# Attention with routed clusters, then a Fourier gate: the first head pair set ahead of the Fourier tables

## The chip, the cores and the metric

The kernel runs on one core of one Trainium2 chip. A core has five engines that work side by side: TensorE (PE) multiplies matrices and loads its weights beside that (PEld), VectorE (DVE) and ScalarE (ACT) work on elements and empty the accumulation banks, GpSimd (POOL) does small things in on-chip memory, and SyncE (SP) issues transfers. ACT and POOL can issue transfers too. The metric is the device time of one launch in microseconds (us), the median of several runs; lower is better. Profile times count from the first instruction of one profiled execution.

## The reference

There are 4 batches of 8 heads, 768 positions of 64 numbers. Each position of q and of k is assigned to one of 16 centroids of its head, by the largest cosine. Attention is allowed only between positions of the same centroid. The result, 768 x 512 per batch, goes through a projection to three parts, a circular convolution of the second with a filter (by Fourier transform), a product with the other two parts and an output projection.

```python
mask = q_assign[:, :, :, None] == k_assign[:, :, None, :]
scores = np.where(mask, scale * np.matmul(q, k.transpose(0, 1, 3, 2)), -1e9)
attn = softmax(scores); x = heads_side_by_side(np.matmul(attn, v))
x1, x2, x3 = split(x @ w_proj)
x2_conv = irfft(rfft(x2) * rfft(filter_fft))
out = (x1 * x2_conv * x3) @ w_out
```

## The kernel before, in words

**Attention.** Heads come in groups n of four (two groups to a batch), each in two pairs pr = 0, 1. A pair takes six steps sk, one for each 128 keys. A step has three score products of 512 columns (L660, issued by `product` as one matmul of 128 weight columns, L72, or two of 64, L74), three exponentials on ACT into one of five p buffers (L669, L672), eight matmuls of P.V into a bank pair (L683), and an addition of p on DVE for the row sums (L697). The mask rides inside the score product: 16 rows below q and k hold the centroid as a one-hot row, times a large number for q, so that unequal centroids give a hugely negative score. These rows are the tiles `augm`; the 64 rows of data are `aug`, cast to bf16.

**Routing.** For each group the q and k tiles are loaded (L295), transposed by PE (L556, or L566 for groups 0 and 1), copied out, multiplied with normalised centroids (`sim`), transposed back, and turned into one-hot rows by five DVE operations. For group 0 this is `first_masks` (L467): once per pair, the keys (j = 1) and queries (j = 0) of both heads together. Pair 0's rows are written by PE transposes and copies (L511, L520); pair 1's go through a tile `ohT` and four transfers issued by SP (L462).

**Fourier tables.** `angles` (L337) makes 768-point angles on DVE with exact rounding, and their sines on ACT into `fw`. `tables` (L375) transposes them into `inv`, loads the filter (L381), and works out the filter's spectrum (L418 to L440). Before, the sines are among the first things on ACT, and every first exponential is made to wait for the last of them by `after=sins`. The second half of the kernel, `hyena` (L785), uses `fw`, `inv` and the spectrum `hm` for each batch.

**The order.** Nothing is ordered by hand. `build` lists some 1,900 operations with the engines that may run them, an estimated duration, a due time and their data dependencies. `Plan.place` (L113) then simulates the engines: of the operations that are ready at about the earliest time, it takes on each engine the one with the smallest due time, with bonuses for staying with P.V and penalties for changing the column mode of PE. Each engine's instructions are issued in the order that comes out. Due times follow a raster: `T0` for the first step, `TAU1` per step for the first 28 and `TAU2` after. `NUDGE` adds a correction to the due time of single operations by their number in the list. A load is not issued earlier than `LEAD` ahead of its due time. Transfers of group 0's heads may go by SP or by ACT; the rest by SP, in order.

```python
o.due += NUDGE.get(o.seq, 0.0)
if o.kind == "load":
    o.ready = max(o.ready, o.due - LEAD)
T0 = 20.38450
TAU1 = 2.97769
```

Of the kernel before, what the change touches and what calls it, by code (L numbers as in the profile page):

```python
# [75 lines left out]

class Plan:

    def __init__(self):
        self.ops, self.writers, self.reads = [], {}, {}

    def op(self, eng, fn, due, r=(), w=(), alloc=None, free=(), lock=False, byts=0, after=(), kind=None, lat=0.0):
        o = Op()
        o.eng = eng if isinstance(eng, dict) else {eng[0]: eng[1]}
        o.fn, o.due, o.alloc, o.free, o.lock, o.byts, o.kind = fn, due, alloc, free, lock, byts, kind
        o.seq = len(self.ops)
        o.due += NUDGE.get(o.seq, 0.0)
        o.outs, o.end, o.start, o.on = [], None, None, None  # L90
        deps, o.soft = set(after), set(after)
        o.lat = lat
        for key in r:
            deps.update(self.writers.get(key, ()))
        for key in w:
            deps.update(self.writers.get(key, ()))
            deps.update(self.reads.get(key, ()))
        for key in r:
            self.reads.setdefault(key, []).append(o)
        for key in w:  # L100
            self.writers[key] = [o]
            self.reads[key] = []
        deps.discard(o)
        o.deps = deps
        o.left = len(deps)
        for d in deps:
            d.outs.append(o)
        for h in free:
            h.readers += 1
        self.ops.append(o)  # L110
        return o
# [107 lines left out]
def banks_for(bank, free, st, o):  # L219
# [14 lines left out]
    elif st.o == st.otiles:  # L234
        if st.tail:
            allowed += [4, 5]
        elif whole(4, 6) < 1e8:
            first += [4, 5]
    t = lambda i: whole(4, 6) if i in first else free[i]
    ids = sorted((i for i in allowed + first if free[i] < 1e8), key=lambda i: (t(i), i))[:bank.n]  # L240
    return (tuple(ids), max(map(t, ids))) if len(ids) == bank.n else None


def build(T):

    P = Plan()
    op = P.op
    T0 = 20.38450
    TAU1 = 2.97769
    TAU2 = 3.43320  # L250
    NE = 28

    def ring(n, pr):
        return (2 * n + pr) % 3

    def A(i):
        return T0 + TAU1 * min(i, NE) + TAU2 * max(i - NE, 0)

    def copy(e, out, in_):
        if e == "ACT":  # L260
# [915 lines left out]
```

## Time and profile before

| | |
|---|---|
| runs shown, median (lowest to highest) | 387.03 us (386.67 to 388.61), 3 runs |
| profiled execution: span | 385.4 us (its own device time is not listed; the median lies 1.6 us above the span) |
| PE busy | 367.3 us |
| DVE busy | 352.3 us |
| ACT busy | 273.1 us |
| POOL busy | 46.6 us |
| first matmul, first exponential, end of the last matmul | 5.11, 22.39, 381.0 us |

The page of a profile gives busy time per engine and, in its fourth part, the chain of work that ended last, followed back from the end. A view by stage gives busy time in chosen stretches. The timeline lists instructions in order of time, merged where like follows like: start, duration, engine, line, operation, output <- input, partitions x elements, count, and in brackets the idle time before and what ended it. PE counts as busy while any matmul is in flight, so a busy PE can be a slow one; the duration of equal instructions tells.

### The profile page before, as it was taken

The page shows a single profiled execution, that of the slowest core. Times are in us where ns is not written, and L with a number is a line of the kernel's source. Part 1 is how long each engine was busy: PE and PEld are TensorE (multiplying, and loading weights), DVE is VectorE, ACT ScalarE, POOL GpSimd, SP SyncE. Part 2 cuts the span into 40 slices and gives each one's busy share as a digit, 9 for nine tenths or more (in the row PEclk, how much of TensorE's full clock was granted, in tenths as well). Part 3 has the DMA queues.
Part 4 walks back from the last instruction along what each step waited for, and adds up shares of the span by engine and source line. Part 5 has one row for each costly group of instructions (what it writes and reads, how often), then busy time and mean ns, then how long its engine had stood idle before and what let it go on. Part 6 is the DMA issues. An engine that isn't in the chain of part 4 may idle for free.

```text
span 385.4 us, 8486 instructions
## 1 busy us (share of the span) xinstructions
PE 367.3 (95%) x3262; PEld 207.6 (54%) x3267; DVE 352.3 (91%) x504; ACT 273.1 (71%) x519; POOL 46.6 (12%) x92
## 2 busy tenths in 40 slices
PE   2999899999999999989999999999999999999995
PEld 1564345445655555556555555555455566555682
DVE  8898988998798999998899999999998999999883
ACT  5897987887894979577975967687867367532342
POOL 8602000000012010101010100101010100000400
PEclk9999999999999999999999999999999999999999
DMA  9819984730679669767886896645657551010214
GB/s 176 196 52 216 215 182 120 170 72 22 166 146 187 119 119 143 121 113 126 161 104 174 144 246 108 119 88 91 102 102 198 62 115 43 4 43 2 101 67 163
DMA packets 93860, 47.17 MB, mean 122 GB/s; under 512 B 82088, under 2 KB 87676, under 8 KB 93820
## 3 DMA queue, kind: packets, MB, share of 16 engines
q1 hardware_dynamic: 87836, 36.84, 42.5%
q0 software_dynamic: 2704, 8.98, 16.0%
q10 hardware_dynamic: 3280, 0.82, 1.2%
q8 instruction: 25, 0.41, 0.5%
q14 instruction: 15, 0.12, 0.1%
HBM read 31.59 MB, written 7.40 MB: 101 GB/s over the span
## 4 chain that ended last, share of the span: by engine, by line
PE 65%; DVE 19%; ACT 6%; issue 4%; DMA 3%; SPq 1%; POOL 0%; DVEq 0%; ACTq 0%; POOLq 0%
PE bank L74 24%; PE pair L683 21%; DVE acc L697 6%; PE bank L809 5%; PE bank L72 4%; PE bank L556 3%; ACT p L672 2%; PE bank L586 2%; DMA dr<-dn 2%; DMA aug<-ohT 2%; ACT aug L261 2%; DVE tm L833 2%; PE bank L599 1%; PE bank L451 1%; PE bank L566 1%
## 5 line engine op out<-in xcount | busy, mean ns | idle before, releaser
L683 PE MATMUL pair<-p,vraw 128*64 128x385 f32 x768 | 142.5, 490 | 0.2
L672 ACT ACTIVATE p<-bank 128x512 f32<-128x512 f32 x192 | 113.7, 613 | 34.1 <-PE bank L74 29.3
L697 DVE TENSOR_TENSOR acc<-p,acc 128x1536 f32<-128x1536 f32 x64 | 112.0, 1750 | 3.9 <-ACT p L672 1.5
L683 PEld LDWEIGHTS pair<-p,vraw 128*64 128x64 f32 x768 | 54.2, 136 | 47.8 <-issue 41.1
L74 PE MATMUL bank<-aug,aug 128*64 128x512 bf16 (+3 forms) x580 | 68.4, 328 | 2.1 <-ACT p L672 1.2
L669 ACT ACTIVATE p<-bank 128x512 f32<-128x512 f32 x96 | 58.6, 611 | 6.2 <-PE bank L74 5.6
L74 PEld LDWEIGHTS <-aug 128*64 128x64 bf16 (+1 forms) x580 | 34.4, 109 | 34.5 <-issue 22.4
L731 POOL DMA_DIRECT2D acc<-acc x30 | 23.6, 788 | 242.6 <-DMA acc<-acc 90.3
L74 PE MATMUL bank<-xT,wpj 128*64 128x384 bf16 x440 | 42.7, 326 | 0.0
L261 ACT COPY qkT<-bank 128x384 f32<-128x384 f32 x63 | 28.1, 497 | 10.5 <-PE bank L74 8.9
L74 PEld LDWEIGHTS <-wpj 128*64 128x64 bf16 x440 | 25.5, 109 | 15.9 <-issue 6.4
L697 DVE TENSOR_TENSOR acc<-p,p 128x1536 f32<-128x1536 f32 x16 | 28.0, 1751 | 3.3 <-ACT p L672 3.1
L74 PEld LDWEIGHTS <-y 128*64 128x64 bf16 x464 | 22.9, 110 | 12.6 <-issue 4.4
L261 ACT CAST aug<-qkT 64x768 bf16<-64x768 f32 x33 | 27.3, 829 | 2.5 <-PE bank L74 1.7
L833 DVE TENSOR_TENSOR tm<-bank,hm 128x512 f32<-128x512 f32 x44 | 27.7, 678 | 0.1
L809 PE MATMUL bank<-wpj,xT 128*64 128x512 bf16 x192 | 21.9, 379 | 0.0
L74 PE MATMUL bank<-wout,y 128*64 128x512 bf16 x176 | 21.1, 379 | 0.0
L72 PE MATMUL bank<-aug,aug 80*128 80x256 bf16 (+3 forms) x92 | 20.0, 321 | 0.2
L556 PE MATMUL bank<-ident,qkraw 128*128 128x128 f32 x144 | 19.6, 279 | 0.3 <-DVE sd L898 0.3
L556 PEld LDWEIGHTS bank<-ident,qkraw 128*128 128x128 f32 x144 | 15.6, 140 | 6.9 <-issue 4.5
L261 ACT COPY tm<-bank 128x512 f32<-128x512 f32 x13 | 7.4, 589 | 15.8 <-PE bank L809 12.0
L701 ACT COPY osb<-pair 128x770 f32<-128x770 f32 x16 | 12.9, 809 | 6.9 <-PE pair L683 6.8
(150 smaller groups left out, 433.0 us busy)
## 6 DMA issues: line engine op xcount, KB each, us to landing
vraw<-in_v_dram SPq DMA_DIRECT2D x16, 384.0 KB, 4.3
qkraw<-in_q_dram SPq DMA_DIRECT2D x30, 192.0 KB, 4.1
qkraw<-in_k_dram SPq DMA_DIRECT2D x30, 192.0 KB, 4.1
rb<-dr SPq DMA_DIRECT2D x30, 192.0 KB, 3.7
out_dram<-ob SPq DMA_DIRECT2D x11, 512.0 KB, 3.0
acc<-acc POOLq DMA_DIRECT2D x10, 384.0 KB, 6.2
acc<-acc POOLq DMA_DIRECT2D x10, 192.0 KB, 4.2
y<-in_moe_filter_fft_dram SPq DMA_DIRECT2D x4, 384.0 KB, 7.1
```

The lines of the kernel that those rows point to most:

```text
L72: return T.nc.tensor.matmul(out, lhsT, rhs, start=start, stop=stop)
L74: T.nc.tensor.matmul(out[64 * i:64 * i + 64], lhsT[:, 64 * i:64 * i + 64], rhs, start=start, stop=stop)
L261: T.nc.scalar.copy(out, in_)
L556: T.nc.tensor.transpose(bank(h.ids[i // 3])[:, ts(i % 3, 128)], raw(s, i), T.ident)
L669: T.nc.scalar.activation(o, ap(h).rearrange("p (a b) -> p a b", a=2), Act.Exp, scale=0.125)
L672: T.nc.scalar.activation(flat(s)[:, lo:lo + 512], ap(h), Act.Exp, scale=0.125)
L683: T.nc.tensor.matmul(o[64 * hp:64 * hp + 64, ch, :385], T.vraw[vs][:, hp, sk * D:(sk + 1) * D], T.p[slots[sk]][:, hp, 384 * ch:384 * ch + ...
L697: T.nc.vector.tensor_tensor(T.acc[os], P_(t[0]), P_(t[1]) if len(t) == 2 else T.acc[os], op=Alu.add)
L701: op(("ACT", .83), lambda e: T.nc.scalar.copy(T.osb[o3], two(ob)[:, :, :385]), te, r=[ob], w=[("osb", o3)], free=[ob])
L731: op(("POOL", .8), lambda e, rows=rows: T.nc.gpsimd.dma_start(flat_()[:rows], flat_()[rows:2 * rows], accum_op=Alu.add), te, r=[], w=[("ac ...
L809: T.nc.tensor.matmul(ap(h)[64 * i:64 * i + 64], T.xT[xs][:, kt, c:c + 64], T.wpj[:, kt, DM:2 * DM], start=kt == 0, stop=kt == ND - 1)
L833: op(("DVE", .68), lambda e, i=i, cs=cs, r=r, h=h: T.nc.vector.tensor_tensor(T.tm[r][:, cs], ap(h), hmrow(i, (0, 2, 2, 3)[2 * r + cs]), op ...
```

## The change

Six things change.

1. *Loads.* The four head loads of pair 0 come first, two on SP and two on ACT; pair 1's four go to SP, with later due times. The loads of the following groups and of the filter no longer wait for the first masks.
2. *Centroids.* A dummy square root and, after the real one, a dummy exponential are put on ACT, so that their function tables are loaded there. The first exponential depends on the latter instead of on the sines.
3. *First masks.* `first_masks(pr, js)` works for pair 0 once for the keys and once for the queries, each with both halves of the positions in one bank, and for pair 1 once for both. The factor of the query rows moves into the constant that marks ties, so that the rows come out by one subtraction (queries) or comparison (keys). Pair 1's masks take eight transfers instead of four.
4. *Angles, sines, tables.* They are listed after the first pair's attention. The angles wait for the first exponential; all sines are one operation on ACT, with the table loads for sine and back to exponential, after the sixth exponential. Tables, filter loads and spectrum get due times relative to `T0`.
5. *Constants.* `T0` is 13.0. Two zero fills of pair 0's tiles go to DVE; the column constants of the old masks go.
6. *Order.* `NUDGE` has 1,911 entries (mean size 133 us) instead of 271 (mean size 2.4 us). A new table `ONLY` pins 160 operations to one engine: 98 to ACT, 51 to DVE, 11 to POOL.

```diff
-NUDGE = {6:-0.2,9:0.7,10:3.7,11:-0.3,71:-0.3, ...
+NUDGE = {0:11.4019,1:487.416,2:-43.9661,3:160.599, ...
+ONLY = {9:"POOL",10:"POOL",11:"POOL",39:"POOL",40:"POOL",50:"DVE",54:"DVE",56:"ACT", ...
...
+        if o.seq in ONLY:
+            o.eng = {ONLY[o.seq]: o.eng[ONLY[o.seq]]}
...
-    T0 = 20.38450
+    T0 = 13.0
...
+    ANG, SINES, LOADF, TAB = T0 + 6, T0 + 10, T0 + 14, T0 + 20
...
-        return [op({"SP": .8, "ACT": .8} if n == 0 else ("SP", .8), lambda e, hp=hp: dma(e)(
+        return [op(("ACT" if hp and (n, pr) == (0, 0) else "SP", .65), lambda e, hp=hp: dma(e)(
...
-        sq = op(("ACT", 1.5), lambda e: T.nc.scalar.activation(cen.s0, cen.ss, Act.Sqrt), 2.4, r=["ss"], w=["s0"])
+        op(("DVE", .1), lambda e: V().memset(T.warm, 1.0), -3, w=["warm"])
+        op(("ACT", 1.45), lambda e: T.nc.scalar.activation(T.warm, T.warm, Act.Sqrt), 1.0, w=["warm"])
+        sq = op(("ACT", .2), lambda e: T.nc.scalar.activation(cen.s0, cen.ss, Act.Sqrt), 2.4, r=["ss", "warm"], w=["s0"])
+        ex = op(("ACT", 1.45), lambda e: T.nc.scalar.activation(T.warm, T.warm, Act.Exp), 2.5, w=["warm"], after=[sq])
...
+        def sines(e):
+            A_ = T.nc.scalar.activation
+            for m, n, r in todo:
+                A_(T.fw[:, :, m, 192:], n(), Act.Sin, scale=sc)
+                A_(T.fw[:, :, m, :192], r(), Act.Sin, scale=sc, bias=T.half_pi)
+            A_(T.ph[:, 0], T.kp, Act.Sin, scale=-math.pi / S, bias=T.half_pi)
+            A_(T.ph[:, 1], T.kp, Act.Sin, scale=math.pi / S)
+            A_(T.warm, T.half_pi, Act.Exp)
+        op(("ACT", 6.5), sines, SINES, r=keys + ["kp", "half_pi"], w=[("fw", m, cs) for m in range(3) for cs in range(2)] + ["ph", "warm"],
+           after=[exps[5]])
...
-    def first_masks(pr):
+    def first_masks(pr, js):
...
+        def pick(e):
+            for z in js:
+                x = oh().rearrange("p (t j m) c -> p t j m c", j=w_, m=4)[:, :, z - js[0]]
+                y = m2().rearrange("p (t j m) -> p t j m", j=w_, m=4)[:, :, z - js[0]]
+                V().tensor_tensor(x, x, y.unsqueeze(3).to_broadcast([128, 3, 4, NC]), op=Alu.is_equal if z else Alu.subtract)
...
-                        free=[h], after=sins if first[0] is None else [first[0]], kind="exp")
+                        free=[h], after=[warm] if first[0] is None else [first[0]], kind="exp")
...
-    for z in range(4):
-        load_qk(0, z // 2, z % 2, .3 + z * .1)
-    sins = angles(sq)
-    got = routing(0)
-    load_v(0, 0, 2.0)
-    for z in range(4):
-        load_qk(1, z // 2, z % 2, 9 + z)
-    load_v(0, 1, 20)
-    tables(got)
+    for z in range(2):
+        load_qk(0, 0, z, .3 + z * .1)
+    load_v(0, 0, 8.0)
+    for z in range(2):
+        load_qk(0, 1, z, 6.5 + z * .1)
+    routing(0)
+    for z in range(4):
+        load_qk(1, z // 2, z % 2, 12 + z)
+    load_v(0, 1, 18)
     for n in range(NG):
-        attention(n, 0, sins)
+        attention(n, 0)
+        if n == 0:
+            angles()
+            tables()
```

## The prediction

> **What bounds the kernel now.** I read the first page for the busy shares, then the busy time by stage, then the timeline of the first 25 us engine by engine, and last the chain of work that ended last. From the page:
>
> ```profile
> span 385.4 us, 8486 instructions
> PE 367.3 (95%) x3262; PEld 207.6 (54%) x3267; DVE 352.3 (91%) x504; ACT 273.1 (71%) x519; POOL 46.6 (12%) x92
> PE 65%; DVE 19%; ACT 6%; issue 4%; DMA 3%; SPq 1%; POOL 0%; DVEq 0%; ACTq 0%; POOLq 0%
> ```
>
> TensorE (PE) is busy 95% of the span and carries 65% of the chain; VectorE (DVE) is close behind. A busy PE may still be a slow one, so the stages come next: start and length, then the busy time of PE, PE's weight loads, DVE, ScalarE (ACT) and GpSimd (POOL), granted clock, DMA share, GB/s.
>
> ```profile
> 0.00:5.11 5.11, 0.00 (x1) 0.03 (x1) 3.61 (x13) 0.78 (x1) 4.18 (x25) 1.00 0.60 134
> 5.11:10.21 5.10, 2.38 (x9) 1.61 (x9) 4.90 (x11) 4.55 (x9) 4.88 (x15) 1.00 1.31 233
> 10.21:22.40 12.19, 12.19 (x96) 7.54 (x97) 10.79 (x23) 10.77 (x22) 5.39 (x13) 1.00 0.74 172
> 22.40:100.00 77.60, 74.68 (x578) 38.30 (x579) 67.33 (x84) 64.73 (x126) 2.61 (x5) 1.00 0.62 134
> 100.00:350.00 250.00, 247.05 (x2190) 139.82 (x2190) 239.97 (x335) 180.36 (x342) 24.46 (x31) 1.00 0.63 118
> 350.00:385.40 35.40, 30.99 (x398) 20.32 (x394) 25.66 (x43) 11.86 (x23) 5.08 (x4) 0.98 0.23 90
> ```
>
> From 22.4 us, where the first exponential starts, to 350 us PE idles 2.92 + 2.95 us in all. So the time is PE's work plus what PE loses at the two ends. The start, as the timelines give it:
>
> ```profile
> 4.33 1.28 ACT L315 ACT_TABLE_LOAD   x1 [4.33 <-issue]
> 5.85 1.28 ACT L358 ACT_TABLE_LOAD   x1
> 15.81 1.28 ACT L372 ACT_TABLE_LOAD   x1
> 22.39 0.58 ACT L672 ACTIVATE p<-bank 128x512 f32<-128x512 f32 x1
> ...
> 5.11 1.51 PE L566 MATMUL bank<-ident,qkraw 128*128 128x128 f32 x6 [5.11 <-DMA qkraw<-in_q_dram]
> 7.61 0.87 PE L566 MATMUL bank<-ident,qkraw 128*128 128x128 f32 x3 [0.99 <-DMA qkraw<-in_k_dram]
> 10.21 0.42 PE L326 MATMUL bank<-ident,sd 128*64 128x128 f32 x1 [1.73 <-DVE sd L323]
> 12.48 2.76 PE L477 MATMUL bank<-qkT,cbd 128*32 128x384 f32 x8
> 16.67 1.48 PE L477 MATMUL bank<-qkT,cbd 128*32 128x384 f32 x8
> ```
>
> Keys land at 7.6 us; centroids are normalised only by 10.2, because DVE works on the angles in between; similarities come at 12.5; and the sine work on ACT (7.1 to 17.3) stands before the first exponential by an explicit dependency. The same eight similarities take 2.76 us, then 1.48: PE runs slowly at first, although the granted clock reads 1.00. The transposes of L566, first those of 5 to 12 us, then those of 18 to 24 us (min/median/max in ns), say the same:
>
> ```profile
> L566 PE MATMUL bank<-ident,qkraw x17: 417/421/448, 5.1 to 11.9; 128*128 128x128 f32 x17
> L566 PE MATMUL bank<-ident,qkraw x15: 272/273/328, 18.3 to 22.3; 128*128 128x128 f32 x15
> ```
>
> **The change part by part.** The start in PE's ledger first. By 22.4 us PE has done, at later rates: 39 transposes at 0.122 us (L556, 12 in 1.46 us) = 4.8; 16 similarities at 0.089 (16 of L586 in 1.43) = 1.4; the small transposes L487 (0.58 per six), L393 (0.33 per three) and L511 (24 in 0.84) = 3.3; the rest 0.6. That is 10.1 us of work, so PE is 12.3 us behind.
>
> *Loads.* Four head loads (q and k of pair 0, 192 KB each) now stand first, two on SP and two on ACT; before, eight shared the 16 DMA engines. At the 217 GB/s that the trace shows from 3 to 9 us, four take 3.6 us from about 2.5, so keys land at 6.1; the upper bound is 7.6, as now. Three issues on ACT instead of five free it at 1.16 + 0.65 + 0.67 = 2.5 instead of 4.3. SP issues the rest: the second pair's four, v, then the next heads' eight, 0.65 each, 9 us of a queue that idles from 18.0 to 25.07 now. The eight mask issues in place of four add 4 x 0.63 = 2.5 us there; what waits behind them, the filter loads and the third heads' loads, is used from 45 us on. No charge; if that cover is gone, 2.5.
>
> *Centroids.* The square root's table (1.28) loads while the centroids fly, so the root is out near 4.1 instead of 5.8. The five small DVE operations that follow (8.28 to 10.16 now) lose the angles from between them: about 1.2 us. Transpose 0.42, two copies 0.45: ready by 6.9, before the keys' transposes are copied out. Nothing is added to the chain.
>
> *First mask.* From keys at 6.1: two groups of three transposes at the slow 0.87 each, 7.9; copy 0.48, 8.4; four similarities, half of 2.76, 9.8; copy 0.47, 10.3; transposes 0.4, 10.7; five DVE operations on half as many elements, between half and all of 0.55 + 0.56 + 0.36 + 0.55 + 0.56 = 2.6, I take 1.6 for 12.3; the queries' own five stand partly in between, +0.7, 13.0; row transposes 0.3, copy 0.8, score 0.4, gaps 0.2: first exponential at 14.7, 7.7 earlier. By then PE has done 12 transposes (1.5), similarities and small transposes 2.1, the rest 0.6, and in its waits the second pair's 12 (1.5) and six of the next heads' (0.7): 6.4 us, so it is 8.3 behind. **Gain 12.3 - 8.3 = 4.0 us.** The other 3.7 us of the 7.7 are PE work that is still to be done, and PE has no idle time behind it to hide it in.
>
> *Angles and sines.* Twelve DVE operations cost 7.9 us now, 0.36 to 0.98 each, the long ones beside POOL's memsets; undisturbed 3 x (0.36 + 0.36 + 0.56 + 0.56) = 5.5. DVE idles 10.3 us from 22.4 to 100, which covers them; uncovered they cost 5.5. The sines become one block on ACT among the exponentials: 3 x 0.52 + 3 x 0.62 + 0.30 + 0.19 + two table loads 2.56 + 0.20 = 6.7 us. The bounds are 0 and 6.7. Covered are up to four filled p buffers at 1.30 us of P.V each, 5.2; I take 6.7 - 5.2 = **+1.5**. The Trainium skill ("ScalarE: Activation LUTs", What ACT_TABLE_LOAD costs) states a further 1.38 us of drain per switch of set; by that the block would last 9.4 us and the sum would be 2.7 us higher; the trace disagrees where it can be seen, the load at 5.85 starts 0.02 us after the root ends at 5.83.
>
> *Memsets and small things.* Two zero fills move from POOL (0.79) to DVE in the first 2 us, where DVE waits 1.34 us for the identity; the DVE price is not in the trace, between 0.15 and 0.56 (its shortest operation and the cast of that shape). Off the path, nothing.
>
> *The order.* The list of due-time corrections grows from 271 small entries (2.4 us in the mean) to one for nearly every operation (133 us in the mean), and 160 operations are pinned to one engine. Every choice among ready operations can differ. What can be priced is the column mode of PE: a P.V step of eight takes 1.30 us after its like and 1.45 after another mode, as the chain shows:
>
> ```profile
> 138.68 2.17 PE bank L72 x13
> 140.85 1.45 PE pair L683 x8
> 142.51 1.30 PE pair L683 x8
> ```
>
> I count 85 changes of mode between 0 and 345 us in PE's timeline, 48 of them before 130 us; after that 11 or 12 in each 70 us. The bounds: all of the early excess gone, 28 x 0.15 = -4.2; the count doubled, 85 x 0.15 = +12.8. Neither end is near to a row, but the early stretch is the one that is rebuilt, and it has the room; I take half of the lower, **-2.1**. PE's idle time of 5.9 us in the middle I leave.
>
> Sum, against the profiled execution: 385.4 - 4.0 + 1.5 - 2.1 = 380.8 of span. The profiled execution lists its span alone; the 1.6 us from there to the median of the runs (387.03) I take as what lies around the span: **382.4**.
>
> **The rivals.** (B) *The whole 7.7 us are kept.* From 36.7 to 52 us the chain runs through ACT and DVE (four aug casts of 0.83, a 1.75 accumulate, the filter's scalings), not PE; if these two set the early pace, all shifts. Against: PE idles only 2.9 us up to 100. 387.0 - 7.7 + 1.5 - 2.1 = 378.7. (C) *The sine block is uncovered:* scores stop, P.V has nothing in stock; all 6.7 are paid: 387.6. For: ACT is busy 64.7 of 77.6 us there. (E) *PE stays slow.* It works in short pieces up to 14.7 us, so the slow pace (421 against 273 ns) may last into the first scores; it lasted some 7 us from PE's first matmul before, and if 5 us of them fall behind the first score at half rate, that is +2.5: 384.9. The Trainium skill ("TensorE: Matmul & The Clock Gate", Part 1) gives such a rule: half clock until a window of about 3.4 us has been busy. The trace agrees, as PE turns fast between 12 and 15 us only. (D) *Slower than before: the new order changes column mode more often*, all along the span. Without the -2.1 the sum is 384.5; it passes 389.0 with (389.0 - 384.5) / 0.15 = 30 more changes; with 50 it gives 392.0, doubled 397.3. For it speaks that 250 us of the span are at 99% PE, where a rearrangement can hardly win; against, that the modes' price is among what the planner weighs.
>
> **How the numbers follow.** Likeliest (A) 0.38, own range 380 to 385; B 0.21; C 0.10; E 0.08; D 0.23. About 0.5% (1.9 us) is what a measurement of this kernel tells from no change. Faster (below 385.1): 0.36 + 0.21 + 0.04 = 0.61; within: 0.02 + 0.08 + 0.03 + 0.01 = 0.14; slower (above 389.0): 0.02 + 0.01 + 0.22 = 0.25. The range reaches below B by its bounds on loads and order (2.5 us), 376, and into D up to 55 more changes, 393; left out are some 0.05 below and 0.12 above.
>
> **What would show it.** Right: first exponential at 13.5 to 16 us, keys' transposes at about 6; similarities of the first pair at the slow price; a sine block of 6 to 7 us on ACT with two loads of 1.28, PE idle 1 to 2 us around it; PE idle from 100 to 350 still near 3 us. Wrong: a first exponential after 18 us; PE idle above 6 us between 100 and 350, or many more P.V steps at 1.45, or a tail after 350 us longer than 35.4.

## The result and the profile after

The changed kernel takes **401.05 us** (median, 399.4 to 402.69) against 387.11 us for the kernel before (386.67 to 388.61): a ratio of 1.036, 95% interval 1.032 to 1.040. It is slower by 14 us where 4.6 us less was forecast, and lies above the range. The profiled execution took 401.85 us. From its page, span, busy shares and the shares of the chain of work that ended last:

```profile
span 399.8 us, 8466 instructions
...
PE 371.3 (93%) x3274; PEld 207.6 (52%) x3274; DVE 361.7 (90%) x529; ACT 266.8 (67%) x503; POOL 44.0 (11%) x85
...
PE 62%; DVE 23%; DMA 5%; issue 4%; ACT 3%; SPq 1%; DVEq 0%; ACTq 0%
```

The span grew by 14.4 us: TensorE (PE) is idle 28.5 us in place of 18.1 (+10.4) and busy 371.3 in place of 367.3 (+4.0) with nearly the same matmuls (3,274 recorded, before 3,262). VectorE (DVE) and DMA grew in the chain. By stage (start and length, busy time of PE, weight loads, DVE, ScalarE (ACT), GpSimd (POOL), granted clock, DMA share, GB/s), cut where the queries land, where the similarities begin, at the first exponential, and at 100 and 350 us:

```profile
0.00:5.44 5.44, 0.00 (x1) 0.03 (x1) 3.63 (x18) 2.90 (x5) 4.42 (x28) 1.00 0.63 130
5.44:8.69 3.25, 3.17 (x13) 2.42 (x14) 1.53 (x5) 0.65 (x2) 0.98 (x3) 1.00 1.39 218
8.69:18.22 9.53, 8.02 (x74) 5.07 (x74) 7.33 (x16) 6.31 (x13) 5.29 (x7) 1.00 1.28 252
18.22:100.00 81.78, 71.30 (x525) 35.56 (x523) 69.52 (x96) 61.73 (x120) 4.45 (x15) 0.94 0.63 124
100.00:350.00 250.00, 244.50 (x2127) 136.10 (x2127) 236.35 (x329) 182.00 (x343) 23.80 (x30) 1.00 0.61 119
350.00:399.80 49.80, 44.35 (x543) 28.43 (x539) 43.31 (x70) 13.26 (x26) 5.04 (x4) 0.99 0.19 73
```

The middle of the table holds the news: from the first exponential to 100 us PE is idle 10.5 us, where it was 2.9 from 22.4 us on, and the clock falls to 0.94. After 350 us nothing is slower, there is only more left: from the last P.V matmul to the end it is 46.5 us (353.3 to 399.8), before 46.9.

How far the work has come says where it is lost. One step is eight P.V matmuls, one key tile of one head pair; its 96 starts, some of them, from PE's timeline (us):

```
step            0     4     8     12    16    24     40     60     76     end
before        25.5  36.8  52.6  63.6  73.8   96.6  147.4  219.3  273.0  385.4
after         26.6  37.0  51.9  72.1  83.8  106.1  158.4  228.5  281.9  399.8
```

Level up to step 8, and 8.5 us behind by step 12. From step 76 to the end another 5.5 us are lost (117.9 us against 112.4), of which PE is idle for 2.4 us; a step is not all that PE does, and no run tells what the rest is. Between steps 8 and 12 stands this, from the timelines of SP, DVE, ACT and PE (start, duration, operation, in brackets the idle time before it and what ended it):

```profile
41.34 9.32 SPq L643 DMA_TRANSPOSE ohT<-oh  x1
...
50.71 0.64 SPq L738 DMA_DIRECT2D dd<-den  x1
...
55.66 0.59 SPq L740 DMA_DIRECT2D dn<-dd  x1
...
57.84 0.23 DVE L759 RECIPROCAL dn<-dn 128x12 f32<-128x12 f32 x1 [8.55 <-DMA dn<-dd]
...
62.24 0.69 ACT L441 ACTIVATE tm<-bank,hw 128x512 f32<-128x512 f32 x1 [7.52 <-DVE hm L445]
...
63.58 1.54 PE L568 MATMUL bank<-ident,qkraw 128*128 128x128 f32 x6 [6.32 <-DVE tm L443]
```

SP hands out transfers one after another, and one of them, the transfer that transposes the one-hot, takes 9.32 us to hand out. Behind it wait the two transfers that carry the softmax denominators out and back, the second of which also waits 4.3 us for the first to land; DVE stands at their reciprocal for 8.55 us with everything else that it has to do queued behind; ACT waits for DVE, and PE for both. In the kernel before, in the same views, this instruction took 3.68 us, later on, and the reciprocal, which stands four accumulations later in DVE's order, waited for nothing:

```profile
37.78 7.67 SPq L295 DMA_DIRECT2D qkraw<-in_q_dram  x2
45.55 3.68 SPq L629 DMA_TRANSPOSE ohT<-oh  x1
...
60.53 0.23 DVE L744 RECIPROCAL dn<-dn 128x12 f32<-128x12 f32 x1
```

SP was held there too, though. The first line is two q loads, and the second of them took 6.86 us to hand out, so that SP came free at 49.23 us, against 50.66 now; the first denominator transfer left even later, at 51.38 us against 50.71. So the hold as such is not new. What is new is an order that wants the results of these transfers sooner.

What SP met is on POOL's queue: all four loads of wpj and the load of wout are issued from 37.98 to 41.15 us, 4.2 MB by the program's count, just ahead of the transpose. In the kernel before the four wpj loads left at nearly the same time, from 36.58 us, and wout at 115.86 us. The kernel's own planner had meant otherwise: in its reckoning the changed kernel's last wpj load stood at 77.5 us and wout at 102.5. But no instruction holds a load until its planned time; it goes as soon as POOL comes to it, and in the new order no instruction that waits stands ahead of wout.

After this gap PE is also slow. By stretches of 4 us:

```profile
56.00:60.00 4.00, 1.26 (x10) 0.35 (x6) 2.05 (x3) 0.00 (x0) 0.00 (x0) 1.00 0.10 26
60.00:64.00 4.00, 0.42 (x2) 0.42 (x3) 4.00 (x5) 1.73 (x4) 0.00 (x0) 0.58 0.32 75
64.00:68.00 4.00, 4.00 (x18) 1.64 (x20) 3.98 (x4) 2.03 (x4) 0.00 (x0) 0.57 0.57 148
```

PE works 1.68 of the 8 us up to 64 us. The granted clock reads 1.00 up to 60.6 us, 0.50 from 60.7 to 67.4 and 1.00 again from 67.5, so that it stays low for 3.9 us after PE is busy again at 63.58: the P.V step at 65.05 us takes 2.68 us in place of 1.30 to 1.5. The clock was also low at the first P.V (26.56 us, 2.83 us, clock 0.50 to 0.52 until 30 us). Busy time times the missing clock, 4.00 x 0.43 + 1.44 x 0.50 + 2.00 x 0.48, makes an estimated 3.4 of the 4.0 us by which PE's busy time grew. Not all of it is lost time: from step 0 to step 8 it takes 25.3 us here, and as long in the kernel with held loads below, where the first P.V ran at the full clock. The Trainium skill ("TensorE: Matmul & The Clock Gate", Part 1) says that the clock drops to half after an idle window of about 3.4 us and comes back after a busy one. The trace agrees after the gap, where PE had been idle for 3.3 us when the clock fell; it does not at the first P.V, where PE had worked 6.0 of the 8.3 us before and was never idle for more than 1.0.

The start itself, from the timelines of ACT, PE, POOL and DVE:

```profile
4.11 1.28 ACT L322 ACT_TABLE_LOAD   x1
...
5.44 1.51 PE L578 MATMUL bank<-ident,qkraw 128*128 128x128 f32 x6 [5.44 <-DMA qkraw<-in_q_dram]
...
7.25 1.51 PE L578 MATMUL bank<-ident,qkraw 128*128 128x128 f32 x6
...
8.69 1.50 PE L488 MATMUL bank<-qkT,cbd 128*32 128x384 f32 x8
...
12.20 3.46 POOL L267 CAST aug<-qkT 64x768 bf16<-64x768 f32 x4 [1.56 <-ACT qkT L265]
...
12.36 1.58 DVE L510 TENSOR_TENSOR oh<-oh,revc 128x192 bf16<-128x192 bf16 x2
...
14.62 1.25 DVE L519 TENSOR_TENSOR oh<-oh,m 128x192 bf16<-128x192 bf16 x2
...
18.22 0.61 ACT L686 ACTIVATE p<-bank 128x512 f32<-128x512 f32 x1
...
26.56 2.83 PE L698 MATMUL pair<-p,vraw 128*64 128x385 f32 x8 [0.98 <-ACT qkT L265]
```

The lines show that centroids and similarities come sooner, as forecast. Then DVE's two bf16 products take 0.79 and 0.62 us each on half-size tiles, while POOL casts beside them. The first exponential leads by 4.2 us (18.22 against 22.39), the first P.V lags by 1.0 (26.56 against 25.54): it starts 8.3 us behind the first exponential, where it was 3.2.

### The profile page after: what moved, and what is told of

It is laid out like the page before. It is cut to its first block, busy times and chain, and to the rows that moved or that the text cites. A ratio compares the mean times of both kernels' runs of the same rounds, so it can differ in the third digit from the quotient of the medians.

```text
span 399.8 us, 8466 instructions
## 1 busy us (share of the span) xinstructions
PE 371.3 (93%) x3274; PEld 207.6 (52%) x3274; DVE 361.7 (90%) x529; ACT 266.8 (67%) x503; POOL 44.0 (11%) x85
## 4 chain that ended last, share of the span: by engine, by line
PE 62%; DVE 23%; DMA 5%; issue 4%; ACT 3%; SPq 1%; DVEq 0%; ACTq 0%
PE bank L75 26%; PE pair L698 20%; DVE acc L712 8%; PE bank L824 4%; PE bank L73 3%; PE bank L568 3%; DVE aug L267 2%; PE bank L599 1%; DMA rb<-dr 1%; PE bank L458 1%; DMA dp<-dd 1%; DMA dd<-den 1%; PE bank L726 1%; DVE tm L848 1%; DMA qkraw<-in_q_dram 1%
## 5 line engine op out<-in xcount | busy, mean ns | idle before, releaser
L698 PE MATMUL pair<-p,vraw 128*64 128x385 f32 x768 | 144.6, 496 | 1.0 <-ACT qkT L265 1.0
L686 ACT ACTIVATE p<-bank 128x512 f32<-128x512 f32 x192 | 110.3, 603 | 26.1 <-PE bank L75 21.3
L683 ACT ACTIVATE p<-bank 128x512 f32<-128x512 f32 x96 | 57.4, 602 | 10.0 <-PE bank L75 8.2
L75 PEld LDWEIGHTS <-aug 80*64 80x64 bf16 (+1 forms) x616 | 36.9, 109 | 36.3 <-issue 25.4
L75 PE MATMUL bank<-xT,wpj 128*64 128x384 bf16 x416 | 37.4, 326 | 0.0
L265 ACT COPY qkT<-bank 128x384 f32<-128x384 f32 x59 | 26.8, 493 | 11.8 <-PE bank L75 5.9
L75 PEld LDWEIGHTS <-wpj 128*64 128x64 bf16 x416 | 23.8, 110 | 13.4 <-issue 4.0
L265 ACT CAST aug<-qkT 64x768 bf16<-64x768 f32 x31 | 25.7, 829 | 1.5 <-PE bank L75 0.8
L265 ACT COPY ob<-bank 128x512 f32<-128x512 f32 x14 | 8.2, 589 | 19.9 <-PE bank L75 18.2
L265 ACT COPY x<-bank 128x384 f32<-128x384 f32 x22 | 10.6, 480 | 13.5 <-PE bank L75 9.3
L73 PE MATMUL bank<-aug,aug 80*128 80x512 bf16 (+3 forms) x76 | 16.9, 322 | 2.1 <-DVE oh L623 0.6
```

Source lines behind the costliest of these rows:

```text
L73: return T.nc.tensor.matmul(out, lhsT, rhs, start=start, stop=stop)
L75: T.nc.tensor.matmul(out[64 * i:64 * i + 64], lhsT[:, 64 * i:64 * i + 64], rhs, start=start, stop=stop)
L265: T.nc.scalar.copy(out, in_)
L683: T.nc.scalar.activation(o, ap(h).rearrange("p (a b) -> p a b", a=2), Act.Exp, scale=0.125)
L686: T.nc.scalar.activation(flat(s)[:, lo:lo + 512], ap(h), Act.Exp, scale=0.125)
L698: T.nc.tensor.matmul(o[64 * hp:64 * hp + 64, ch, :385], T.vraw[vs][:, hp, sk * D:(sk + 1) * D], T.p[slots[sk]][:, hp, 384 * ch:384 * ch + ...
```

## The experiments

In the diffs `move(list, before)` takes planned operations, by their number, out of the written order and puts them ahead of another one. Numbers of interest in the changed kernel: 158 the first reciprocal, 159 to 161 the transfers behind it, 330 the copy at L1015, 333, 331, 332 and 334 the wpj loads, 335 wout, 76, 82, 81 and 75 POOL's casts for the second pair.

### The stall: the reciprocal's place, and the loads ahead of it

```diff
+    move([158, 159, 161, 160], 318)
```


> Only the order is touched: the reciprocal of the first pair's row sums on DVE, which sat 8.55 us waiting for its transfer at 49.3 us, is issued behind some ten later DVE operations, and the three transfers that follow from it go with it. Theory Q (a stalled queue: DVE is held by one small operation, and PE and ACT run dry behind it): DVE's idle time from 49 to 58 us goes, PE's 6.3 us of idle time at 57 us goes, and the time falls by 6 to 8.5 us, to 392.5 to 395 against 401.05. Theory W (the loss is more DVE work and a worse order all along; the stall is slack that is made up later): at most 2 us, 399 or more.

Measured: 399.78 us (398.0 to 402.48; ratio 1.032, 1.026 to 1.038). The wait moved: step 12 starts at 66.5 us, 5.6 sooner, but the transpose is still held 8.60 us, PE then waits 1.90 us for mask rows, and DVE 4.71 us for the late reciprocals' broadcast (rb). So it is the transfers that come late, and a later place on DVE only moves the wait. The forecast, 392.5 to 395, missed.

```diff
-T.nc.gpsimd.tensor_copy(T.wpj[0:1, :, 0:1], T.f[1][0:1, 0, 0:4].unsqueeze(2))
+T.nc.gpsimd.tensor_copy(T.wpj[0:1, :, 0:1], T.dn[0:1, 0:4].unsqueeze(2))
...
+    move([330, 333], 294)
```


> The weight loads on POOL (four of 768 KB and one of 1 MB, 38 to 41 us) now wait for the reciprocal of the first pair; nothing else moves. Theory Q1 (SP's transposing transfer takes 9.32 us to issue because these 4 MB are in flight beside it, and the row-sum transfers stand behind it on SP): the transpose's issue falls to 4 us or less, the reciprocal waits 2 us or less, and the time is 393 to 396. Rival Q2 (the transposing transfer is slow for its own sake or because of the head loads before it): its issue stays at 8 to 9 us and the time at 400 to 402.

Measured: **396.05 us** (394.25 to 396.71; ratio 1.021, 1.016 to 1.025), 5.0 below the changed kernel. In SP's and DVE's timelines the hold and the wait are gone:

```profile
43.00 1.34 SPq L643 DMA_TRANSPOSE ohT<-oh  x1
...
51.04 0.22 DVE L759 RECIPROCAL dn<-dn 128x12 f32<-128x12 f32 x1
```

DVE's idle time between step 0 and step 12 falls from 10.1 to 1.9 us. With the loads out of the way the stall is gone.

Both together, with the reciprocal moved as in the first, and the copy that waits for it and one load (333) put ahead of 159:

```diff
...
+    move([158, 159, 161, 160], 318)
+    move([330, 333], 159)
```


> Both at once. If the two act on the same loss (theory Q with Q1), no more than the better of the two alone, 391 to 395. If they are two losses, the sum of the two gains. Theory W: 398 or more.

Measured: 399.32 us (398.5 to 401.12; ratio 1.031, 1.026 to 1.035). But this run is not the sum of the two. In POOL's order the other loads of wpj now stand ahead of the copy: two of the four left at 37.47 and 38.24 us as before, and the transpose was held 3.76 us. Further on DVE waits 1.34 us for the broadcast and PE 3.31 us for a k load. Whether the two edits would add is not shown.

### Which load, and whether it does the same in the kernel before

```diff
+    move([335], 665)
```


> The order after the change with one instruction put elsewhere on GpSimd's queue: wout's load (1.05 MB by the program's count) goes behind the first two adds into acc in memory, where it stood before (issued at 115.9 us there, at 40.3 us in the changed kernel); the four loads of wpj stay where they are. Theory W1 (wout is the last straw: the transposing transfer is issued at 41.34 us, 0.2 us behind wout's, and SP is held until much of the 4.2 MB has landed): the issue of the transpose falls from 9.3 to 5 to 7 us, the reciprocal of the denominators waits 4 to 6 us in place of 8.55, and the time is 397 to 399 us. Theory W2 (wpj alone does it): the issue stays at 8.5 us or more and the time within 1 us of the changed kernel's 401.

Measured: 400.40 us (398.25 to 401.68; ratio 1.032, 1.028 to 1.037). The issue stays at 8.92 us, so wpj's four loads are enough to hold SP; the reciprocal waits 4.80 us. Each theory is half right, and the time doesn't tell it from the changed kernel.

In the kernel before, the loads are 329 to 332 and wout is 333:

```diff
+    move([330, 331, 332, 333], 254)
```


> The kernel before, with wout's load right behind wpj's four, as the chip has it after the change (issued near 39 us in place of 115.9). If the stall is made by the loads on GpSimd's queue whatever the rest of the kernel does, it appears here too: the transposing transfer, issued at 45.55 us and 3.7 us long with wpj's 3.1 MB seven to nine us old, takes 5 to 8 us, what stands behind it on SP (a k load, den's transfer, eight mask rows) is 1.5 to 4 us later, and the time is 388 to 391 us. Rival: at 45.5 us most of the bytes have landed, the issue stays under 4.5 us, and the time is within 1 us of 387.2: then it is where the two meet that counts, not the order on GpSimd alone.

Measured: 391.67 us (388.92 to 393.98; ratio 1.010, 1.007 to 1.014). One load placed 77 us earlier in an otherwise unchanged kernel makes the same picture and costs 4 us (timelines of POOL, SP and DVE):

```profile
38.45 0.82 POOL L1008 DMA_DIRECT2D wout<-in_moe_w_out_dram  x1
...
45.32 6.57 SPq L629 DMA_TRANSPOSE ohT<-oh  x1
...
63.45 0.23 DVE L744 RECIPROCAL dn<-dn 128x12 f32<-128x12 f32 x1 [3.25 <-DMA dn<-dd]
```

In most kernels SP is let go near a landing on POOL's queue (transfer records, us). Of the names, wout_behind and before_wout_early are the two kernels just told, recip_and_weights and weights_held those of the part before; the others come below: casts_later, before_held and before_spread with casts or loads moved, before_plain and after_plain in the planner's plain order.

```
                    transpose issued, released    weight load landed just before or after
before                  45.55      49.23          fourth wpj   48.85
after                   41.34      50.66          fourth wpj   50.39  (wout 54.08)
wout_behind             41.76      50.68          fourth wpj   50.78
casts_later             38.93      47.21          fourth wpj   46.94  (wout 50.23)
before_wout_early       45.32      51.88          wout         51.96
before_spread           40.92      43.55          first wpj    42.80
before_plain            39.84      49.15          fourth wpj   48.77
recip_and_weights       41.59      45.35          second wpj   44.62
weights_held            43.00      44.35          none in flight
before_held             40.23      42.40          none in flight
after_plain             46.27      47.61          none near (fourth wpj 48.05, wout 50.59)
```

The last row speaks against the landings alone: two of POOL's loads are in flight, and the transpose is handed out in 1.34 us all the same. There SP had issued no head load since 33.91 us. What the transfers moved while the transpose was held tells more (POOL's queue q0 and SP's queue q1: packets, MB, share of the 16 engines; first the changed kernel, then weights_held, then after_plain):

```profile
q0 software_dynamic: 859, 1.69, 96.6%
q1 hardware_dynamic: 680, 0.17, 13.7%
...
q1 hardware_dynamic: 687, 0.17, 56.3%
...
q0 software_dynamic: 166, 0.26, 106.0%
q1 hardware_dynamic: 30, 0.00, 3.8%
```

In the first two SP's own head loads, issued just before, are still moving: 0.17 MB of them, which take 9.32 us beside POOL's 1.69 MB and 1.34 us alone. In the third SP has next to nothing left to move. So the long hold goes with both together, unfinished loads of SP's own and POOL's large ones that slow them. What exactly SP waits for, and so why it is the fourth load in some and wout in another, is not settled.

### The start

```diff
+    for o in order:
+        if o.seq in [39, 40, 58, 75, 76, 81, 82]:
+            o.on = "ACT"
```


> The seven casts of the first heads that POOL does run on ACT at the same places in the order, so that POOL no longer works beside DVE's one-hot operations. Those took 0.79 us each for the product with the constant against 0.36 for twice the elements before. Theory C (POOL beside DVE lengthens the first mask): the two products fall to about 0.25 us each and the first exponential comes at 16.5 to 17.3 us instead of 18.2. For the time: if what PE lags at the start is carried to the end, 399.5 to 400.5; if the later stall swallows it, 401.

Measured: 401.27 us (400.38 to 403.22; ratio 1.036, 1.030 to 1.042). The products fall to 0.43 us for two, but on ACT the casts (2.52 us for three at 9.24) stand ahead of the similarities' copy, and the first exponential comes at 20.46 us, later than without the edit. So the casts were left on POOL and made to wait for the one-hot, here with the weights held:

```diff
...
+    move([76, 82, 81, 75], 106)
...
+    x76.fn = (lambda f: lambda e: (T.nc.gpsimd.tensor_copy(T.wpj[0:1, 0, 0:2], T.oh[0:1, 0, 11:13, 0]), f(e)))(x76.fn)
```


> The changed kernel with the weights held (396.05 us), and GpSimd's four casts for the second head pair waiting until the first pair's one-hot is made, so that they no longer run beside VectorE's bf16 products (1.58 and 1.25 us for two each beside them). Theory C2 (the casts slow these products, and the start of the path counts): the products take 0.4 to 0.8 us for two, first exponential 1.5 to 2.5 us sooner after the first key transposes, time 394 to 395.5 us. Rival B (the lead is not used): the exponentials come sooner, the first P.V and the end do not; 395.5 to 397 us.

Measured: **392.78 us** (391.43 to 394.14; ratio 1.013, 1.009 to 1.018), 3.3 below the held kernel, more than either side gave. From the timelines of DVE and PE, the products and the first P.V:

```profile
13.10 0.43 DVE L510 TENSOR_TENSOR oh<-oh,revc 128x192 bf16<-128x192 bf16 x2
...
14.21 0.62 DVE L519 TENSOR_TENSOR oh<-oh,m 128x192 bf16<-128x192 bf16 x2
...
25.72 1.52 PE L698 MATMUL pair<-p,vraw 128*64 128x385 f32 x8 [0.98 <-ACT qkT L265]
```

0.43 against 1.58, 0.62 against 1.25. The Trainium skill ("GPSIMD Engine Reference", 8. Key points) names such contention for DVE instructions with two inputs from SBUF; the trace agrees, and the comparison that reads a bank (L508) takes 0.61 us for two with and without the casts. The first P.V came 2.7 us sooner than in the held kernel (28.40; 0.8 of it because the similarities began sooner in this execution, at 8.77 us against 9.53), step 12 2.6 us sooner and the end of the span 3.1 (391.3 against 394.4).

The later casts alone, with the loads where the change puts them:

```diff
+    move([76, 82, 81, 75], 106)
...
```


> The changed kernel with GpSimd's four casts for the second pair made to wait until the first pair's one-hot is done, and nothing else: the weights' loads stay where the change has them. If the start and the stall are two separate losses, the start's gain of 3.3 us shows here as well and the time is 397 to 398.5 us. Rival: a sooner start only lets the transposing transfer meet the loads sooner, SP is held until the same moment, and the time stays within 1 us of 401.

Measured: 396.91 us (396.03 to 397.85; ratio 1.024, 1.021 to 1.026), 4.1 below the changed kernel. The start (4.1), the loads (5.0) and both (8.3) add up to within a microsecond: two separate losses.

An earlier first P.V alone, with the loads held:

```diff
...
+    move([240], 134)
+    move([112], 233)
+    move([119], 139)
+    move([127], 141)
```


> The changed kernel with the weights' loads held behind the first reciprocal (396.05 us so far), and in it the first three P.V steps placed earlier in TensorE's order, with the one ScalarE copy that frees the first one's bank placed ahead of four exponentials. Theory L (the 4 us by which the exponentials lead are lost because the written order keeps the first P.V behind ten exponentials and a bank): the first P.V starts about 3 us earlier relative to the first exponential than the 8.3 us of the held kernel, TensorE's idle time up to the second P.V falls by 1 to 2 us, no gap is followed by a P.V of over 2 us, and the time is 393 to 395 us. Rival B (from the first exponential on ScalarE and VectorE are full, 4.55 and 4.50 of 4.6 us between 22.0 and 26.6, so the lead cannot be turned into P.V whatever the order): P.V starts earlier but the twelfth step of it does not, and the time is within 1 us of 396.

Measured: 395.82 us (394.85 to 396.12; ratio 1.021, 1.017 to 1.025), not told from the held kernel. The first P.V stands 6.9 us behind the first exponential in place of 8.3, but step 12 starts at 65.7 us as it did (65.8). The end of the span came 0.5 us sooner, though the first P.V came 2.2 us sooner. From the first exponential on ACT and DVE are full (4.60 and 4.46 of 4.6 us between 22.0 and 26.6), which fits rival B: P.V can't run ahead of them.

### The written order

Both kernels with the table of corrections, and the table of pinned engines, empty:

```diff
-NUDGE = {0:11.4019,
...
+NUDGE = {}
+ONLY = {}
```


> The changed kernel with its table of due-time corrections and pinned engines emptied, so that the planner orders the work by its rules alone; the computation is the same. To be read against the plain order of the kernel before, in this same set. Theory S (the loss lies in the structure: loads and key paths as the change arranges them): plain after is slower than plain before by 10 us or more. Theory O (the loss lies in the one order that the change wrote down): the two plain kernels lie within 5 us of each other, or this one is faster. The planner's own spans are 408.9 us here against 396.8, so by its estimate +12.

> The kernel before with its table of due-time corrections emptied; the computation is the same. By the planner's estimate 396.8 against 383.5 with the table, so 397 to 404 us on the chip, 10 to 17 over the kernel before. It is the other half of the comparison of plain orders: structure loses if the plain order after the change is 10 us or more above this one, order loses if the two are within 5.

Measured: 417.49 us (413.13 to 419.63) and 401.51 us (399.95 to 402.76), ratios to the kernel before 1.073 and 1.036. The 16 us between them answer the number of theory S, not its reason. In the plain order after the change the transpose is held only 1.34 us; instead PE waits 6.22 us at 32.9 us for a table row that waits for the late sines, and the first P.V starts at 43.99 us although the first exponential is at 18.6. The plain order of the kernel before has the long hold, 9.31 us beside wpj's loads alone. So the two plain orders lose in other places than the two written ones, and whether structure or order costs the time is not decided by them; they show that the plain rules serve the new structure worse.

Twenty late copies and casts that the change pins to DVE, given to ACT, with the weights held:

```diff
+    for o in order:
+        if o.seq in [613, 1027, 1299, 1300, 1304, 1305, 1312, 1314, 1315, 1507,
+                     1512, 1517, 1583, 1592, 1593, 1842, 1891, 1894, 1901, 1909]:
+            o.on = "ACT"
```


> The changed kernel with the weights held (396.05 us), and twenty copies and casts of the later stages that the change pins to VectorE given to ScalarE, which is idle 7 to 18 us in every stretch of about 45 there, while VectorE's idle time is under 4. If VectorE's added load makes the loss that is left after 100 us (TensorE idle 4.8 us from 101.6 to 348 against 2.2 before), up to 2.5 us comes back: 393.5 to 395 us. If not, the time is within 1 us of 396, or longer where the copies push exponentials back.

Measured: 394.88 us (394.02 to 396.66; ratio 1.019, 1.015 to 1.024). 1.2 us less, inside the spread of both: not shown.

### Where the loads could go

The kernel before, its four wpj loads held behind the first reciprocal by the same change to the copy ahead of them:

```diff
...
+    move([328, 329, 330], 320)
```


> The kernel before with its four wpj loads held in the same way, behind the first reciprocal of the denominators. If the transposing transfer's 3.7 us there is made of the same wait on transfers in flight, its issue falls to about 1.3 us, what stands behind it on SP is 2.3 us sooner, and TensorE's idle time between the first P.V and the twelfth step, 2.2 us, can fall by 1 at most: 385.5 to 387 us, the fastest of all kernels here. Rival: nothing waits for it there, and the time is within 0.7 us of 387.3; the loads then land 20 us later than now and may meet other transfers, which would show as a longer time.

Measured: 395.07 us (394.65 to 395.29; ratio 1.019, 1.014 to 1.023), 7.6 us slower, far from the gain and further than the rival's bound; that rival's last clause is what happened. The transpose is handed out in 2.18 us, but the loads now leave at 61.7 us and meet the second round of denominators, whose reciprocal comes at 76.36 us in place of 70.17. From the timelines of POOL, SP and PE:

```profile
61.73 2.51 POOL L1005 DMA_DIRECT2D wpj<-in_moe_w_proj_dram  x4 [0.32 <-POOL wpj L1002]
...
71.09 3.27 SPq L295 DMA_DIRECT2D qkraw<-in_q_dram  x1
...
83.92 1.54 PE L556 MATMUL bank<-ident,qkraw 128*128 128x128 f32 x6 [4.74 <-DVE oh L609]
```

A plain load, the q load of the second line, is held as well, for 3.27 us. The loads one at a time, each behind an accumulation on DVE, with the later casts:

```diff
...
+    move([331], 350)
+    move([332], 374)
+    move([334], 465)
+    move([335], 388)
...
+        x.fn = (lambda f: lambda e: (T.nc.gpsimd.tensor_copy(w(), T.acc[os][0:1, 0, 0:4]), f(e)))(x.fn)
```


> The held kernel with the later casts (392.78 us), and the weights' five loads no longer in one batch but one at a time, each behind a later accumulation on VectorE (about 48, 57, 67, 86 and 92 us). Theory W (the batch of 4.2 MB, wherever it is issued, delays small transfers and loads): TensorE's wait of 1.5 us for a k load at 70 us and the 2.5 us issue of den's transfer at 60 us go, and the time is 390 to 392 us. Rival N (the rest is the written order's many small waits): these waits go but are replaced, and the time is within 1 us of 392.8.

> The same with the twenty late copies and casts on ScalarE (they gave 1.2 us with the weights held). If the three causes are independent, 1 us below the kernel with spread loads, 389 to 391 us, still 2 to 4 us above the kernel before: then the rest is the written order. Rival: with the loads spread, the copies push exponentials back and the time is the same or longer.

Measured: 398.39 us (397.59 to 401.07; ratio 1.030, 1.026 to 1.034) and 398.98 us (397.2 to 400.79; ratio 1.029, 1.025 to 1.033). At step 28 the first is 1.5 us ahead of the held kernel with later casts (104.9 against 106.4), as theory W had it; then wout alone, 1.05 MB, does it again, as the timelines of POOL, SP, DVE and PE show:

```profile
93.87 0.77 POOL L1021 DMA_DIRECT2D wout<-in_moe_w_out_dram  x1 [0.30 <-POOL wout L1124]
...
95.87 4.56 SPq L299 DMA_DIRECT2D qkraw<-in_q_dram  x2
...
106.83 0.23 DVE L759 RECIPROCAL dn<-dn 128x12 f32<-128x12 f32 x1 [4.09 <-DMA dn<-dd]
...
113.94 1.51 PE L613 MATMUL bank<-ident,sim 128*128 128x128 f32 x6 [3.86 <-DVE sim L267]
```

Without wout there, the same two q loads take 1.29 us. The copies on ACT change nothing here.

In the kernel before, its first load in place and the other three behind accumulations:

```diff
+    move([330], 348)
+    move([331], 372)
+    move([332], 463)
...
```


> The kernel before with its first wpj load where it is (36.6 us) and the other three one at a time behind accumulations at about 57, 68 and 79 us. Holding all four behind the reciprocal made TensorE wait 4.7 us at 83.9 us, where they met den's second round of transfers. If it is the batch that does harm, one at a time does none, the transposing transfer's issue falls from 3.7 to below 2.5 us, and the time is 385.5 to 387.4 us. Rival: any load in that stretch meets a small transfer somewhere, and the time is 388 us or more.

Measured: 388.05 us (386.96 to 389.55; ratio 1.001, 0.999 to 1.003): no difference. The transpose is held 2.62 us in place of 3.68, and nothing gains by it.

Last, wout behind the first adds into acc in memory, with and without the copies on ACT:

```diff
-    move([335], 388)
+    move([335], 665)
```


> The kernel with spread wpj loads and later casts (398.39 us), with wout's load moved behind the first two adds into acc in memory, where the kernel before has it (near 120 us). If the stall at 113.9 us is wout's, SP's issue of the two q loads near 96 us falls from 4.56 to about 1.3 us, the wait of 4.1 us for the reciprocal's values goes, the step at 28 stays at 105 us, and the time is 390 to 392.5 us. If not (the q loads wait for something else), the wait stays and the time is 397 us or more. What is then left above 387.6 is not the weights, the casts or the stall.

> The same with the twenty late copies and casts on ScalarE: 0.5 to 1.5 us less than the kernel beside it if VectorE's load is part of what is left (389 to 391.5 us), within 0.5 us of it if not.

Measured: 395.23 us (392.31 to 398.72; ratio 1.017, 1.013 to 1.022) and 395.43 us (394.97 to 397.45; ratio 1.021, 1.017 to 1.025; the second is called all_parts, the kernel with spread loads and later casts spread_casts). The wait at 113.9 is gone (step 32 starts at 121.3 us in all_parts, 128.0 in spread_casts); in its place PE waits for mask rows. SP hands out the transpose ahead of them in 1.42 us, at 119.02, beside wout, now at 116 us, and then waits 6.3 us for it to land. From all_parts:

```profile
116.43 1.08 POOL L1021 DMA_DIRECT2D wout<-in_moe_w_out_dram  x1
...
127.66 3.70 SPq L470 DMA_DIRECT2D aug<-ohT  x6
...
131.40 0.41 PE L75 MATMUL bank<-aug,aug 80*64 80x512 bf16 x2 [2.79 <-DMA aug<-ohT]
```

So wout was the cause at 113.9 us, and neither of the two later places was free in this order. No version beats the kernel before; the best of the changed ones is the held kernel with later casts, at 392.78.

**What stays open.** That kernel is still some 5 us above the kernel before (ratio 1.013). Its first P.V is level (25.7 against 25.5), so the loss lies behind it: from there to the end 365.6 us against 359.9. PE is idle 14.8 us of that in place of 10.0, in many small waits; the largest, from the list of what PE waited for (total us, times, longest):

```profile
PE bank L568 <- DMA qkraw<-in_k_dram: 1.5, 1, 1.5
PE bank L400 <- DVE inv L267: 1.3, 1, 1.3
PE bank L568 <- issue: 1.2, 1, 1.2
PE bank L613 <- DVE sim L267: 1.2, 1, 1.2
```

Taking one away (spreading the loads) brought another, which speaks for the order as a whole; it was not shown. Nor do the waits tell where most of it comes: by steps this kernel is only 1.3 us behind at step 76 (274.3 against 273.0) and 6.5 at the last P.V matmul (345.1 against 338.5), and PE is idle for 1.6 us more in between.

## Why the prediction was wrong, step by step

Two terms failed. The start was to gain 4.0 us and gained nothing; making POOL's casts wait there gave 4.1. SP's queue was to cost nothing; taking the large loads out of its way gave 5.0. Both repairs together give 8.3 us, and the kernel is still 5.3 us above the kernel before, where 4.6 below was forecast; that rest stays open.

- **Start, "gain 12.3 - 8.3 = 4.0 us": failed.** The first exponential came at 18.22 us, not 14.7, though ahead of 22.39. The mis-sized terms: keys' transposes at 7.25 us, not 6.1 (PE was still at the queries'); the one-hot 4.8 us (11.10 to 15.87), not 1.6 + 0.7; two row copies 1.68, not 0.8. "Between half and all" of the full-size row was no bound: a half-size product cost more than twice the full one (0.79 against 0.36), because POOL's four casts run beside it. The prediction had no price for these casts; making them wait gave 4.1 us back. The ledger also took the first exponential for PE's start. P.V starts 8.3 us behind it, before 3.2, and PE is idle 9.4 us up to the first P.V, before 8.1: no gain. Placing P.V sooner by itself (6.9 us behind) brought nothing; that ACT and DVE are full in between is the likely reason.
- **"SP queue: no charge; if that cover is gone, 2.5": the step that decided.** It asked what waits behind the eight mask issues. It did not ask what the queue's own instructions wait for. The view of SP before the change showed it: 7.67 us for two q loads and 3.68 for a transpose, beside POOL's loads of the weights. These loads were not in the sum at all, and holding them gave 5.0 us. Moving wout alone back behind (400.40 us) is not told from no change, so it is the loads as a whole that count.
- **Order, -2.1: wrong in kind.** There are 81 changes of column mode in the whole span in place of 85, worth -0.6 us, so rival D's mechanism did not happen, though its sign did. As far as the runs show, the order cost time by what it wants sooner behind a held queue, not by modes. No rival had a queue that stands, and so the range ended at 393.
- **Rival E, slow PE: right in kind, wrong in place.** At the first scores PE was fast (0.55 us for three transposes at 10.12 us). The slow clock came later, at the first P.V and after the gap, for an estimated 3.4 us of busy time.
- **Centroids: right in that they add nothing.** The root is out at 4.09 us (near 4.1 forecast), the centroids are normalised at 5.54 and in place at 7.91 (6.9 forecast), still before the keys' transposes are copied out (8.16 us on).
- **Sines, +1.5: covered.** The block runs from 31.87 to 37.83 us, 6.0 us (6.7 forecast), and PE is busy through all of it. Around its two table loads nothing more is lost: the second, at 36.34 us, starts 0.02 us after the last sine.
- **Signs named in advance.** A first exponential after 18 us was one for wrong, and came. PE's idle time from 100 to 350 us, 5.5 us, lies between the two signs. A tail after 350 us longer than 35.4 came too but meant nothing, as everything came later. Of the signs for right, the similarities at the slow price failed as well: eight took 1.50 us.

## What to carry to other kernels

An engine that hands out transfers in order can be stopped in the handing out itself: when a change reorders loads, list for every queue which large transfers are in flight when a small one that something waits for is issued, and check in the trace before when each load really left, since a planned time that no instruction enforces holds nothing. Look for a hold in the kernel before, too: one that costs nothing there can cost when the order behind it changes. Work taken off one chain and put on another engine at the same time is not free when the two slow each other, as POOL's casts and DVE's products did here: price it from a row in which they run side by side. An earlier first operation is worth what the bounding engine's first long run gains by it, no more.

## What the runs showed of the hardware that was not expected

- SP is held while it issues a transfer, and for longer when loads of its own are unfinished and large loads issued by POOL are in flight beside them: the first transposing transfer of a kernel 1.34 to 2.18 us with none of POOL's, 2.62 with one wpj load, 3.68 to 9.32 with two to five. Large loads alone don't hold it: 1.34 us beside two of them when SP had next to nothing of its own left to move (after_plain), and a later one 1.42 beside wout (all_parts). Plain loads are held too: a q load 6.86 us beside wpj's loads, two q loads 1.29 us without and 4.56 us with 1.05 MB of wout in flight.
- SP's head loads moved 0.17 MB in 9.32 us beside 1.69 MB of POOL's loads and in 1.34 us without them.
- Two bf16 products of 128x192 on DVE took 0.43 us alone and 1.58 us beside POOL's casts from fp32 to bf16; two subtractions or comparisons of that size 0.62 and 1.25.
- The granted clock fell to 0.50 when PE had been idle for 3.3 us and came back after 3.9 us of work; a P.V step took 2.68 us in place of 1.30 to 1.5. It also fell after 8.3 us in which PE worked 6.0 us and was never idle for more than 1.0.
